# One decode step of gated attention and a feed-forward layer: the feed-forward projections go from TensorE to VectorE, and part of the first load is cut into other pieces

## The chip, the cores and the metric

The kernel runs on one core of a Trainium2 chip. The metric is device time in microseconds of that core, as the median of three runs. In the profile PE is TensorE, DVE is VectorE, ACT is ScalarE, POOL is GpSimd, and SP is the engine that here issues every DMA (a transfer between main memory and the on-chip memory).

## What is computed

One token `x` of 1024 numbers goes through two branches, and a gate mixes them. All data are 32-bit floats.

```python
g = sigmoid((x * gate_w).sum())
# branch A: 32 query heads of 128, 4 key/value heads, 65536 cached positions
q = x @ wq                       # wq 1024 x 4096
p = softmax(q . k_cache / sqrt(128))
a = (p @ v_cache) @ wo           # wo 4096 x 1024
# branch B: one routed token, so the routing picks it
r = x @ w_r
h = silu(x @ w_gate) * (x @ w_up)    # 1024 x 3584 each
b = x + sigmoid(r) * (h @ w_down)    # w_down 3584 x 1024
out = g * a + (1 - g) * b
```

The caches and the weights are some 346 MB, and each byte is used once.

## The kernel before, in words

Everything is written out by hand on five engines, with semaphores between them. The on-chip memory holds three large buffers of 128 partitions by 16384 columns: `kb` and `vb` (named kbuf and vbuf in the profile) and `wb` (wbuf). SP issues the loads in one fixed order on one queue, and before each load it waits until the buffer's last use is counted (`load`).

The stages, in order:

1. **First load.** `wq0` (128 x 8224: the query weights of the first head group, 8192 columns, and 32 columns that hold `x`, `gate_w` and `w_r`) lands in the second half of `wb`. VectorE forms the gate and spreads `x` into `xp`.
2. **Four head groups** (`G`), each with query weights, four K loads and four V loads of 16384 columns (`NL`), a running softmax on VectorE and ScalarE, and the output projection into the PSUM tile T (`T<-wbuf,op`).
3. **Feed-forward projections.** The loop `Fori(0, 2)` runs once for `w_gate` and once for `w_up`. Each weight comes as two halves of 14336 columns, four rows of the weight's 3584 columns to a partition: one half in `kb`, one in `vb`. TensorE multiplies each half by `xp` in 32 matmuls of 448 columns into the PSUM tile R. ScalarE copies R to `row`, TensorE turns it into columns (7 matmuls into S), and VectorE forms silu in `hid` and, after the second pass, `hp`, the hidden vector as TensorE's operand.
4. **Down projection.** The first 16 of 28 blocks of `w_down` come in one load of 16384 columns (semaphore `s_down`) into `wb`, the other 12 in six pieces (`s_part`) into `kb`. VectorE takes the first `SUMS` = 6 blocks as six multiply-adds over 1024 columns into `t`; TensorE takes the rest into T, and adds `t` by two matmuls with ones (`T<-t,ones`). Blocks from `JOIN` = 24 on go straight into the PSUM tile Y, by 64 columns. T is copied to `join` by VectorE, joined into Y by 16 matmuls, and a transpose on VectorE (`fin`) and one small store end the kernel.

PE waits for other engines at `event()`, a wait on the semaphore `to_pe`, and for loads at `landed(...)` or a plain wait. `k_done`, `v_done`, `att_done` and `FFN + n` are counts of PE's own semaphore that SP and the other engines wait for. TensorE's operations are recorded in the helper `mm` (line 149 of the profile) and SP's loads in `load` (line 111). The lines that matter below: 113 (first load), 126 to 138 (order of the feed-forward loads), 210 to 226 (projections), 361 to 396 (silu, `hp` and the six sums).

Of the kernel before, what the change touches and what calls it, by code (L numbers as in the profile page):

```python
# [14 lines left out]
F = 3584  # L15
NL = 4
W = 16384
KB = D // P
FB = F // P
FR = F // 8  # L20
FQ = FB // 4
SCALE = DH ** -0.5
XN = 32
JOIN = 24
SUMS = 6
R4 = 4
CW = D // 16
PIECES = ((0, 3), (3, 4))


# [17 lines left out]
        self.wait(self)  # L48


def gated_mix(nc, k_t, v_t, wq0, wo_wq, tail, out):
# [18 lines left out]
    kb, vb, wb = sb("kbuf", W), sb("vbuf", W), sb("wbuf", W + XN)  # L70
    t, pt = sb("t", 1024), sb("pt", 1024)
    acc, q_sb, join, row = sb("acc", 512), sb("q_sb", 512), sb("join", 512), sb("row", 2 * FR)
    first = wb[:, W // 2 :]
# [19 lines left out]
    S, R, A, M, T, Y = ps("S", 1024), ps("R", 1024), ps("A"), ps("M"), ps("T"), ps("Y")  # L93
# [6 lines left out]
    k_done = lambda g, i: START + HEAD * g + 2 + 3 * i + 1  # L100
# [4 lines left out]
    FFN = START + HEAD * G  # L105


    def load(dst, src, sem, n=0):
        if n:
            sp.wait_ge(pe.sem, n)  # L110
# [13 lines left out]
    half = KB // 2 * F  # L124
    down = at + 4 * half
    for dst, n, sem, after in (
        (kb, half, s_k, k_done(G - 1, NL - 1)),
        (vb, half, s_v, v_done(G - 1, NL - 1)),
        (kb, half, s_k, FFN + 1),
        (vb, half, s_v, FFN + 2),  # L130
        (wb, W, s_down, att_done(G - 1)),
    ):
        load(dst[:, :n], tail[:, at : at + n], sem, after)
        at += n
    parts = [4 * D, 4 * D, 2 * D, D] + [4 * CW * (r1 - r0) for r0, r1 in PIECES]
    for k, n in enumerate(parts):
        to = at - down - W
        load(kb[:, to : to + n], tail[:, at : at + n], s_part[k], 0 if k else FFN + 4)
# [69 lines left out]


    with p.Fori(0, 2):  # L210
        for b, (buf, sem) in enumerate(((kb, s_k), (vb, s_v))):
            landed(sem)
            for k in range(KB // 2):
                for e in range(2):
                    for j in range(4):
                        c = k * F + (2 * j + e) * FR
                        ins = mm(
                            R[32 * j : 32 * j + 32, 512 * e : 512 * e + FR], xp[:, KB // 2 * b + k, :], buf[:, c : c + FR],
                            b == k == 0, b == 1 and k == KB // 2 - 1,
                        )  # L220
            pe(ins)
# [4 lines left out]
    pe.n = FFN + 6  # L226

    event()
    p.wait_ge(s_down, 16)
    d1 = wb.rearrange("p (b n) -> p b n", n=D)  # L230
    tiles(T, [hp[:, b, 3:35] for b in range(SUMS, 16)], d1[:, SUMS:, :], False, False)
    event()
    tiles(T, [ones[:, :32]], t.unsqueeze(1), False, False)
    for k in range(2):
        p.wait_ge(s_part[k], 16)
        d2 = kb[:, 4 * k * D : 4 * (k + 1) * D].rearrange("p (b n) -> p b n", n=D)
        ins = tiles(T, [hp[:, 16 + 4 * k + b, 3:35] for b in range(4)], d2, False, k == 1)
# [6 lines left out]
    later = kb[:, 8 * D : 11 * D].rearrange("p (b j r n) -> p b j r n", b=3, j=4, r=R4)  # L244
    for b in range(3):
        if b != 1:
            p.wait_ge(s_part[(2, 0, 3)[b]], 16)
        for r in range(R4):
            for j in range(4):
                y_row(j, r, hp[:, JOIN + b, :], later[:, b, j, r, :], b == r == 0)  # L250
        if b == 1:
            event()
            joined = join.rearrange("p (j r n) -> p j r n", j=2, r=R4)
            for r in range(R4):
                for j in range(4):
                    y_row(j, r, selj[:, j // 2, :], joined[:, j % 2, r, :])
# [35 lines left out]
    v.wait_ge(s_x, 16)  # L292
    d(v.tensor_copy(xp[:, :, 0], xk[:, 0, :]))
    d(v.tensor_mul(dots, xk[:, 0:1, :].to_broadcast([P, 2, KB]), xk[:, 1:3, :]))
    dve.own()
    tell_pe(v.tensor_reduce(dsum, dots, AX.X, ALU.add))
    act.wait(pe, 1)
# [60 lines left out]
            xr.unsqueeze(1).unsqueeze(3).to_broadcast([P, 4, KB, 32]),  # L358
        )
    )  # L360
    for u in range(2):
        act.wait(pe, FFN + 3 * u + 2)
# [5 lines left out]
        cols = FFN + 3 * u + 3  # L368
        if u == 0:
            act.wait(pe, cols)  # L370
            act(a.activation(hid, S[:, :FB], AF.Exp, scale=-1.0))
            dve.wait(act)
            d(v.tensor_scalar_add(hid, hid, 1.0))
            dve.own()
            d(v.reciprocal(hid, hid))
            dve.own()
            d(v.tensor_mul(hid, S[:, :FB], hid))
            dve.own()
            d(v.tensor_scalar_mul(hid, hid, rest[:, 1:2]))
        else:  # L380
            dve.own()
            dve.wait(pe, cols)
            tell_pe(
                v.tensor_mul(
                    hp[:, :, 3].rearrange("p (j m) -> p m j", j=4), S[:, :FB].rearrange("p (m j) -> p m j", j=4),
                    hid.rearrange("p (m j) -> p m j", j=4),
                )
            )
    d(v.tensor_mul(hid, S[:, :FB], hid))
    dacc, h = t, hid.rearrange("p (m j) -> p j m", j=4)  # L390
    v.wait_ge(s_down, 16)
    dve.own()
    for b in range(SUMS):
        ins = v.scalar_tensor_tensor(dacc, wb[:, b * D : (b + 1) * D], h[:, 0, b : b + 1], dacc, op0=ALU.mult, op1=ALU.add)  # L394
        if b < SUMS - 1:
            d(ins)
            dve.own()
# [43 lines left out]
```

## Time and profile before

| | us |
|---|---|
| Median of three runs | 805.68 (805.59 to 805.71) |
| The profiled execution's own time | 805.7 |
| Its span, first to last instruction | 804.4 |
| TensorE matmuls busy | 396.7 (49%) |
| VectorE busy | 82.2 (10%) |
| ScalarE busy | 24.9 (3%) |

The profiled execution's time agrees with the median, so its stages can be read as those of the timed runs; 1.3 us of it lie outside the span. A row of the timeline has its start, its length, the engine, the line, the operation, what is written and read, the shape and how many instructions are merged in it; in brackets stands the idle time of that engine just before and what ended it. [...]

### The profile page before, as it was taken

Reading aid. Unit: us, or ns where it says so; the run is one execution under the profiler, and the core shown is the slowest. Engines: PE = TensorE matmul, PEld = TensorE weight load, DVE = VectorE, ACT = ScalarE, POOL = GpSimd, SP = SyncE. Lnnn points to the kernel's source line nnn. Section 1 sums busy time; section 2 is a strip of 40 time slices with the busy share of each in tenths; the row PEclk is TensorE's granted clock in tenths of the full one; section 3 lists DMA queues with packets and bytes.
Section 4 is the critical chain, followed back from the end, with each engine's and each line's share of the span. In section 5 each row is a group of like instructions: output and inputs, shape, how many; then the busy total and the mean of one; then the engine's idle time right before and its main releaser. Section 6 shows DMA issues by size and latency. Waiting matters only on the chain. (4 is left out here: it accounts for less than half of the span.)

```text
span 804.4 us, 6296 instructions
## 1 busy us (share of the span) xinstructions
PE 396.7 (49%) x2932; PEld 124.3 (15%) x2932; DVE 82.2 (10%) x159; ACT 24.9 (3%) x49; POOL 2.7 (0%) x12
## 2 busy tenths in 40 slices
PE   3444554455544444455445455455444454545556
PEld 1111111111111111111111111111111111111222
DVE  1010101010001010100101010100101010100004
ACT  0000000000000000000000000000000000000000
POOL 1000000000000000000000000000000000000000
PEclk9777677677676776776776777777777777777768
DMA  9999999999999999999999999999999999999997
GB/s 415 420 418 466 417 420 466 417 417 463 424 417 460 427 417 460 427 417 460 427 417 456 430 417 453 433 417 450 433 420 443 440 420 430 437 449 417 451 422 320
DMA packets 7061, 346.13 MB, mean 430 GB/s; under 512 B 912, under 2 KB 1040, under 8 KB 1296
## 3 DMA queue, kind: packets, MB, share of 16 engines
q1 hardware_dynamic: 7056, 346.05, 99.4%
q8 instruction: 4, 0.07, 0.0%
q14 instruction: 1, 0.01, 0.0%
HBM read 346.05 MB, written 0.00 MB: 430 GB/s over the span
## 5 line engine op out<-in xcount | busy, mean ns | idle before, releaser
L149 PE MATMUL S<-kbuf,qp 128*32 128x512 f32 x1024 | 145.2, 730 | 155.6 <-PEq L146 155.6
L149 PE MATMUL A<-vbuf,pt 128*32 128x512 f32 x1024 | 145.2, 730 | 132.3 <-PEq L146 132.3
L149 PEld LDWEIGHTS S<-kbuf,qp 128*32 128x32 f32 x1024 | 40.1, 131 | 257.4 <-issue 257.4
L149 PEld LDWEIGHTS A<-vbuf,pt 128*32 128x32 f32 x1024 | 40.1, 131 | 224.4 <-issue 224.4
L322 DVE TENSOR_REDUCE m<-S 128x1 f32<-128x1024 f32 x16 | 19.6, 1224 | 291.3 <-PE S L149 291.3
L149 PE MATMUL T<-wbuf,op 128*32 128x512 f32 x128 | 21.9, 847 | 24.5 <-PEq L146 24.5
L341 DVE SCALAR_TENSOR_TENSOR acc<-acc,alpha,A 128x512 f32<-128x512 f32 x12 | 9.0, 748 | 169.1 <-PE A L149 169.1
L149 PE MATMUL R<-vbuf,xp 128*32 128x448 f32 x128 | 17.6, 721 | 16.3 <-PEq L146 16.3
L149 PE MATMUL R<-kbuf,xp 128*32 128x448 f32 x128 | 17.5, 716 | 15.6 <-PEq L146 15.6
L334 ACT ACTIVATE t<-S,nb 128x1024 f32<-128x1024 f32 x16 | 17.6, 1099 | 196.8 <-DVE nb L327 196.8
L338 DVE STREAM_TRANSPOSE pt<-t 128x1024 f32<-128x1024 f32 x16 | 19.8, 1239 | 5.1 <-ACT t L334 5.1
L149 PE MATMUL M<-mg,heads 128*128 128x16 f32 x32 | 5.9, 259 | 27.3 <-PEq L143 27.3
L333 ACT ACTIVATE alpha<-nb 128x1 f32<-128x1 f32 x12 | 3.5, 294 | 449.5 <-DVE nb L330 449.5
L149 PE MATMUL R<-wbuf,xp 128*32 128x512 f32 x128 | 16.1, 647 | 0.0
L149 PEld LDWEIGHTS T<-wbuf,op 128*32 128x32 f32 x128 | 5.7, 148 | 37.5 <-issue 37.5
L149 PEld LDWEIGHTS M<-mg,heads 128*128 128x128 f32 x32 | 4.8, 188 | 41.4 <-issue 41.4
L149 PE MATMUL T<-wbuf,hp 128*32 128x512 f32 x40 | 6.1, 771 | 7.5 <-DMA wbuf<-in_tail 7.5
L149 PEld LDWEIGHTS R<-vbuf,xp 128*32 128x32 f32 x128 | 5.4, 140 | 28.6 <-issue 28.6
L149 PEld LDWEIGHTS R<-kbuf,xp 128*32 128x32 f32 x128 | 5.4, 140 | 27.1 <-issue 27.1
L149 PE MATMUL T<-join 128*128 128x512 f32 x2 | 2.0, 1126 | 13.9 <-PEq L143 13.9
L343 DVE COPY acc<-A 128x512 f32<-128x512 f32 x4 | 2.8, 691 | 59.7 <-PE A L149 59.7
L394 DVE SCALAR_TENSOR_TENSOR t<-wbuf,hid,t 128x1024 f32<-128x1024 f32 x6 | 7.7, 1285 | 7.3 <-DMA wbuf<-in_tail 7.1
(74 smaller groups left out, 80.5 us busy)
## 6 DMA issues: line engine op xcount, KB each, us to landing
kbuf<-in_tail SPq DMA_DIRECT2D x2, 7168.0 KB, 31.0
vbuf<-in_tail SPq DMA_DIRECT2D x2, 7168.0 KB, 29.5
wbuf<-in_wq SPq DMA_DIRECT2D x1, 4112.0 KB, 12.6
wbuf<-in_tail SPq DMA_DIRECT2D x1, 4096.0 KB, 38.0
kbuf<-in_tail SPq DMA_DIRECT2D x2, 2048.0 KB, 34.3
kbuf<-in_tail SPq DMA_DIRECT2D x1, 1024.0 KB, 38.5
kbuf<-in_tail SPq DMA_DIRECT2D x1, 512.0 KB, 39.3
kbuf<-in_tail SPq DMA_DIRECT2D x1, 384.0 KB, 39.8
```

The lines of the kernel that those rows point to most:

```text
L149: return p.matmul(o, w, r, start=first, stop=last)
L322: d(v.tensor_reduce(m1, S, AX.X, ALU.max))
L333: act(a.activation(alpha, was, AF.Exp, bias=now, scale=-1.0))
L334: act(a.activation(t, S, AF.Exp, bias=now, scale=SCALE, accum_out=sums if i else l1))
L338: tell_pe(v.transpose(pt, t))
L341: d(v.scalar_tensor_tensor(acc, acc, alpha, A, op0=ALU.mult, op1=ALU.add))
L343: d(v.tensor_copy(acc, A))
L394: ins = v.scalar_tensor_tensor(dacc, wb[:, b * D : (b + 1) * D], h[:, 0, b : b + 1], dacc, op0=ALU.mult, op1=ALU.add)
```

## The change

The two passes of the projections are taken from TensorE's weights-times-`xp` form. VectorE now multiplies each of the four weight rows on a partition by that partition's `x` and adds it into `facc` (one 128 x 3584 accumulator, which lies half at the end of `kb` and half at the end of `wb`): one product and seven multiply-adds to a pass, in four steps per half. TensorE only adds the accumulator over the partitions, by 8 matmuls with ones. The third half now goes to `wb` and the fourth to `kb`; the down projection's first load goes to `vb` and its pieces to `wb`. Three of these loads now wait for the count `free`, which VectorE raises at the end of a half. `SUMS` goes from 6 to 7 and `JOIN` from 24 to 26: VectorE sums one block more, and two blocks that went into Y go into T. The sum `t` is added to T after the second piece instead of before the first.

The first load loses its first 640 columns. They come as two further DMAs: 96 partitions, whose source is written as 12 groups of 8 rows, and 32 partitions, written as 8 groups of 4 rows, that land in `t`; VectorE copies the latter to their partitions.

```diff
-    sp.dma_start(first, wq0).then_inc(s_x, 16)
+    first, edge = wb[:, W // 2 + SIDE :], wb[:, W // 2 : W // 2 + SIDE]
+    sp.dma_start(first, wq0).then_inc(s_x, 16)
+    sp.dma_start(edge[:96], side[:96].rearrange("(e q) n -> e q n", e=12)).then_inc(s_side, 16)
+    sp.dma_start(t[:32, :SIDE], side[96:].rearrange("(e q) n -> e q n", e=8)).then_inc(s_side, 16)
...
-        (kb, half, s_k, FFN + 1),
-        (vb, half, s_v, FFN + 2),
-        (wb, W, s_down, att_done(G - 1)),
+        (wb, half, s_ffn[2], att_done(G - 1)),
+        (kb, half, s_ffn[3], used(0)),
+        (vb, W, s_down, used(1)),
...
+        event()
+        for e in range(2):
+            for j in range(4):
+                c = 2 * j + e
+                rhs = facc[:, c // 4, (c % 4) * FR : (c % 4 + 1) * FR]
+                ins = mm(R[32 * j : 32 * j + 32, 512 * e : 512 * e + FR], ones[:, :32], rhs)
+        pe(ins)
...
+    v.wait_ge(s_side, 32)
+    d(v.tensor_copy(edge[96:], t[:32, :SIDE]))
...
+    def rows(u, i, buf):
+        v.wait_ge(s_ffn[2 * u + i], 16)
+        if u and i == 0:
+            dve.wait(pe, FFN + 1)
+        for k in range(KB // 2):
+            src = buf[:, k * F : (k + 1) * F].rearrange("p (i n) -> p i n", i=2)
+            x = xk[:, 0, 4 * i + k : 4 * i + k + 1]
+            if i == k == 0:
+                ins = v.tensor_scalar_mul(facc, src, x)
+            else:
+                dve.own()
+                ins = v.scalar_tensor_tensor(facc, src, x, facc, op0=ALU.mult, op1=ALU.add)
+            if k < KB // 2 - 1:
+                d(ins)
+        return ins
...
+    rows(0, 0, kb).then_inc(free, 1)
+    v.wait_ge(free, 1)
+    rows(0, 1, vb).then_inc(free, 1)
+    v.wait_ge(free, 2).then_inc(to_pe, 1)
+    hidden(0)
+    act.wait(pe, FFN + 2)
+    act(a.activation(hid, S[:, :FB], AF.Exp, scale=-1.0))
+    rows(1, 0, wb).then_inc(free, 1)
...
+    v.wait_ge(free, 3)
+    tell_pe(rows(1, 1, kb))
+    hidden(1)
```

`hidden(u)` is ScalarE's copy of R to `row`, as before. On VectorE, from the end of attention to the sums, the order before is this (L373 to L379 are silu, `hp` and `hid` the hidden vector, and L394 the sums of down-projection blocks):

```order
L355 TENSOR_TENSOR t<-ident,xr 128x1024
L373 TENSOR_SCALAR hid<-hid 128x28 [waits n_act]
L375 RECIPROCAL hid<-hid 128x28 [waits n_dve]
L377 TENSOR_TENSOR hid<-S,hid 128x28 [waits n_dve]
L379 TENSOR_SCALAR hid<-hid,rest 128x28 [waits n_dve]
L384 TENSOR_TENSOR hp<-S,hid 128x7x4 [waits n_pe,n_dve]
L389 TENSOR_TENSOR hid<-S,hid 128x28
L394 SCALAR_TENSOR_TENSOR t<-wbuf,hid,t 128x1024 [waits n_dve,s_down]
```

In the changed kernel the same stretch of VectorE reads as follows (`bufs` is the one tensor that now holds `kb`, `wb` and the accumulator; L377 and L380 are the projections):

```order
L363 TENSOR_TENSOR t<-ident,xr 128x1024
L377 TENSOR_SCALAR bufs<-bufs 128x2x1792 [waits s_ffn0]
L380 SCALAR_TENSOR_TENSOR bufs<-bufs 128x2x1792 [waits n_dve] x3
L380 SCALAR_TENSOR_TENSOR bufs<-vbuf,bufs 128x2x1792 [waits n_dve,s_ffn1,free]
L380 SCALAR_TENSOR_TENSOR bufs<-vbuf,bufs 128x2x1792 [waits n_dve] x3
L377 TENSOR_SCALAR bufs<-bufs 128x2x1792 [waits free,n_pe,s_ffn2]
L380 SCALAR_TENSOR_TENSOR bufs<-bufs 128x2x1792 [waits n_dve] x3
L402 TENSOR_SCALAR hid<-hid 128x28 [waits n_act]
...
L380 SCALAR_TENSOR_TENSOR bufs<-bufs 128x2x1792 [waits n_dve,s_ffn3,free]
L380 SCALAR_TENSOR_TENSOR bufs<-bufs 128x2x1792 [waits n_dve] x3
L415 TENSOR_TENSOR hp<-S,hid 128x7x4 [waits n_pe,n_dve]
```

Sixteen long VectorE instructions now stand ahead of `hp`, with the four of silu between the third and the fourth half. On TensorE the program's end before is this, from the down projection on:

```order
L149 MATMUL T<-wbuf,hp 32x512 [waits to_pe,s_down]
L149 MATMUL T<-wbuf,hp 32x512 x19
L149 MATMUL T<-t,ones 32x512 [waits to_pe]
L149 MATMUL T<-t,ones 32x512
L149 MATMUL T<-kbuf,hp 32x512 [waits s_part0]
L149 MATMUL T<-kbuf,hp 32x512 x7
L149 MATMUL T<-kbuf,hp 32x512 [waits s_part1]
L149 MATMUL T<-kbuf,hp 32x512 x7
L149 MATMUL Y<-kbuf,hp 32x64 [waits s_part2]
L149 MATMUL Y<-kbuf,hp 32x64 x31
L149 MATMUL Y<-join,selj 32x64 [waits to_pe]
```

And this is TensorE's end in the changed kernel:

```order
L161 MATMUL T<-vbuf,hp 32x512 [waits to_pe,s_down]
L161 MATMUL T<-vbuf,hp 32x512 x17
L161 MATMUL T<-bufs,hp 32x512 [waits s_part0]
L161 MATMUL T<-bufs,hp 32x512 x7
L161 MATMUL T<-bufs,hp 32x512 [waits s_part1]
L161 MATMUL T<-bufs,hp 32x512 x7
L161 MATMUL T<-t,ones 32x512 [waits to_pe]
L161 MATMUL T<-t,ones 32x512
L161 MATMUL T<-bufs,hp 32x512 [waits s_part2]
L161 MATMUL T<-bufs,hp 32x512 x3
L161 MATMUL Y<-bufs,hp 32x64 [waits s_part3]
L161 MATMUL Y<-join,selj 32x64 [waits to_pe]
```

The two matmuls on `t` moved behind 16 others; only 4 matmuls of T, and 32 fewer of Y, stand behind them.

## Rows read from the trace of the kernel before

**Rows 1.** The page: the queues of the whole execution, with packets, MB, and the share of 16 DMA engines' span.

```profile
DMA  9999999999999999999999999999999999999997
...
q1 hardware_dynamic: 7056, 346.05, 99.4%
q8 instruction: 4, 0.07, 0.0%
```

**Rows 2.** The chain of waits that ended last, in order of time: start, length, what.

```profile
795.54 4.41 PE T L149 x35
799.96 0.97 PE Y L149 x61
...
802.67 0.25 DVE fin L402
```

**Rows 3.** The timeline of the last 25 us, all engines.

```profile
777.27 0.92 ACT L365 ACTIVATE row<-R 128x896 f32<-128x896 f32 x1 [30.96 <-PE R L149]
...
778.34 1.70 PE L149 MATMUL S<-sel,row 128*128 128x4 f32 x14 [1.12 <-PEq L143]
780.14 0.21 DVE L384 TENSOR_TENSOR hp<-S,hid 128x28 f32<-128x28 f32 x1 [32.76 <-PE S L149]
780.25 0.18 DVE L389 TENSOR_TENSOR hid<-S,hid 128x28 f32<-128x28 f32 x1
787.50 7.89 DVE L394 SCALAR_TENSOR_TENSOR t<-wbuf,hid,t 128x1024 f32<-128x1024 f32 x6 [7.08 <-DMA wbuf<-in_tail]
...
787.52 6.12 PE L149 MATMUL T<-wbuf,hp 128*32 128x512 f32 x40 [7.49 <-DMA wbuf<-in_tail]
...
795.54 0.62 PE L149 MATMUL T<-t,ones 128*32 128x512 f32 x2 [1.90 <-PEq L143]
...
796.02 4.00 PE L149 MATMUL T<-kbuf,hp 128*32 128x512 f32 x30
...
800.10 0.69 DVE L400 COPY join<-T 128x512 f32<-128x512 f32 x1 [4.71 <-PE T L149]
...
800.94 0.65 PE L149 MATMUL Y<-join,selj 128*32 128x64 f32 x32
...
801.38 1.22 PE L149 MATMUL Y<-kbuf,hp 128*32 128x64 f32 x64
```

**Rows 4.** The timeline of PE at the start, from the first K load on: when TensorE could begin on each load.

```profile
32.73 8.92 PE L149 MATMUL S<-kbuf,qp 128*32 128x512 f32 x64 [9.41 <-PEq L146]
...
53.59 8.73 PE L149 MATMUL A<-vbuf,pt 128*32 128x512 f32 x64 [9.87 <-PEq L146]
72.90 9.31 PE L149 MATMUL S<-kbuf,qp 128*32 128x512 f32 x64 [10.58 <-PEq L146]
...
92.20 9.90 PE L149 MATMUL A<-vbuf,pt 128*32 128x512 f32 x64 [7.92 <-PEq L146]
```

**Rows 5.** The timeline of the projections: the four halves on PE, and silu.

```profile
717.57 8.68 PE L149 MATMUL R<-kbuf,xp 128*32 128x448 f32 x64 [10.20 <-PEq L146]
...
734.53 8.73 PE L149 MATMUL R<-vbuf,xp 128*32 128x448 f32 x64 [8.28 <-PEq L146]
...
746.34 0.18 DVE L373 TENSOR_SCALAR hid<-hid 128x28 f32<-128x28 f32 x1 [41.79 <-ACT hid L371]
...
747.14 0.24 DVE L379 TENSOR_SCALAR hid<-hid,rest 128x28 f32<-128x28 f32 x1
...
751.44 8.81 PE L149 MATMUL R<-kbuf,xp 128*32 128x448 f32 x64 [5.36 <-PEq L146]
...
768.30 8.91 PE L149 MATMUL R<-vbuf,xp 128*32 128x448 f32 x64 [8.05 <-PEq L146]
```

**Rows 6.** VectorE's instructions grouped by line and shape over the whole execution: busy us, mean ns of one.

```profile
L394 DVE SCALAR_TENSOR_TENSOR t<-wbuf,hid,t 128x1024 f32<-128x1024 f32 x6 | 7.7, 1285 | 7.3 <-DMA wbuf<-in_tail 7.1
...
L337 DVE SCALAR_TENSOR_TENSOR l<-l,alpha,sums 128x1 f32<-128x1 f32 x12 | 2.6, 220 | 17.5 <-ACT t L334 17.5
...
L345 DVE TENSOR_SCALAR lb<-ones,l 128x128 f32<-128x128 f32 x4 | 1.1, 286 | 0.1
L349 DVE TENSOR_SCALAR rl<-rl,sig 128x8 f32<-128x8 f32 x4 | 0.9, 231 | 0.1
```

**Rows 7.** PE's matmuls grouped by shape in the stretch from 717.5 to 720.5 us, the first 16 of the first half.

```profile
L149 PE MATMUL R<-kbuf,xp 128*32 128x448 f32 x16 | 3.2, 952 | 10.2 <-PEq L146 10.2
```

**Rows 8.** The timeline of SP's queue: when the last loads were issued.

```profile
726.31 0.33 SPq L111 DMA_DIRECT2D kbuf<-in_tail  x1
743.32 0.33 SPq L111 DMA_DIRECT2D vbuf<-in_tail  x1
743.69 0.43 SPq L111 DMA_DIRECT2D wbuf<-in_tail  x1
760.31 2.70 SPq L111 DMA_DIRECT2D kbuf<-in_tail  x6
```

**Rows 9.** The timeline of VectorE after the first load.

```profile
13.34 0.17 DVE L293 COPY xp<-wbuf 128x8 f32<-128x8 f32 x1 [8.51 <-DMA wbuf<-in_wq]
...
23.36 0.21 DVE L315 COPY qp<-M 128x32 f32<-128x32 f32 x1 [1.21 <-PE M L149]
```

More of the change, by code (lines that the diff above doesn't have):

```diff
@@ L23 @@
 XN = 32
-JOIN = 24
-SUMS = 6
+JOIN = 26
+SUMS = 7
 R4 = 4
 CW = D // 16
+SIDE = 640
 PIECES = ((0, 3), (3, 4))
@@ L48, in own, with gated_mix @@
         self.wait(self)
-def gated_mix(nc, k_t, v_t, wq0, wo_wq, tail, out):
+def gated_mix(nc, k_t, v_t, wq0, side, wo_wq, tail, out):
     pe, dve, act, pool = (
@@ L61, in gated_mix @@
     s_part = [nc.alloc_semaphore(f"s_part{i}") for i in range(6)]
+    s_ffn = [nc.alloc_semaphore(f"s_ffn{i}") for i in range(4)]
     def sb(name, *shape):
@@ L69, in gated_mix @@
         sb("gap", (256 - nc.sbuf_base % 256) // 4)
-    kb, vb, wb = sb("kbuf", W), sb("vbuf", W), sb("wbuf", W + XN)
+    bufs, vb = sb("bufs", 2 * W + 2 * XN), sb("vbuf", W)
+    kb, wb = bufs[:, :W], bufs[:, W : 2 * W + XN]
+    facc = bufs[:, : 2 * W].rearrange("p (i n) -> p i n", i=2)[:, :, W - F // 2 :]
     t, pt = sb("t", 1024), sb("pt", 1024)
     acc, q_sb, join, row = sb("acc", 512), sb("q_sb", 512), sb("join", 512), sb("row", 2 * FR)
-    first = wb[:, W // 2 :]
+    first, edge = wb[:, W // 2 + SIDE :], wb[:, W // 2 : W // 2 + SIDE]
+    s_side = nc.alloc_semaphore("s_side")
     xk = wb[:, W : W + 3 * KB].rearrange("p (i k) -> p i k", i=3)
@@ L105, in gated_mix, with used @@
     FFN = START + HEAD * G
+    free = nc.alloc_semaphore("free")
+    def used(i):
+        return free, i + 1
     def load(dst, src, sem, n=0):
         if n:
-            sp.wait_ge(pe.sem, n)
+            sp.wait_ge(*(n if isinstance(n, tuple) else (pe.sem, n)))
         sp.dma_start(dst, src).then_inc(sem, 16)
     sp.dma_start(first, wq0).then_inc(s_x, 16)
+    sp.dma_start(edge[:96], side[:96].rearrange("(e q) n -> e q n", e=12)).then_inc(s_side, 16)
+    sp.dma_start(t[:32, :SIDE], side[96:].rearrange("(e q) n -> e q n", e=8)).then_inc(s_side, 16)
     for g in range(G):
@@ L126, in gated_mix @@
     for dst, n, sem, after in (
-        (kb, half, s_k, k_done(G - 1, NL - 1)),
-        (vb, half, s_v, v_done(G - 1, NL - 1)),
-        (kb, half, s_k, FFN + 1),
-        (vb, half, s_v, FFN + 2),
-        (wb, W, s_down, att_done(G - 1)),
+        (kb, half, s_ffn[0], k_done(G - 1, NL - 1)),
+        (vb, half, s_ffn[1], v_done(G - 1, NL - 1)),
+        (wb, half, s_ffn[2], att_done(G - 1)),
+        (kb, half, s_ffn[3], used(0)),
+        (vb, W, s_down, used(1)),
     ):
@@ L137, in gated_mix @@
         to = at - down - W
-        load(kb[:, to : to + n], tail[:, at : at + n], s_part[k], 0 if k else FFN + 4)
+        load(wb[:, to : to + n], tail[:, at : at + n], s_part[k], 0 if k else used(2))
         at += n
@@ L210, in gated_mix @@
     with p.Fori(0, 2):
[L211 to L221, printed above, removed]
+        event()
[5 more added lines that the diff above has]
+        pe(ins)
         event()
@@ L225, in gated_mix @@
         pe(ins)
-    pe.n = FFN + 6
+    pe.n = FFN + 4
     event()
     p.wait_ge(s_down, 16)
-    d1 = wb.rearrange("p (b n) -> p b n", n=D)
+    d1 = vb.rearrange("p (b n) -> p b n", n=D)
     tiles(T, [hp[:, b, 3:35] for b in range(SUMS, 16)], d1[:, SUMS:, :], False, False)
-    event()
-    tiles(T, [ones[:, :32]], t.unsqueeze(1), False, False)
-    for k in range(2):
+    d2 = wb[:, : 10 * D].rearrange("p (b n) -> p b n", n=D)
+    for k, (b0, b1) in enumerate(((0, 4), (4, 8), (8, 10))):
         p.wait_ge(s_part[k], 16)
-        d2 = kb[:, 4 * k * D : 4 * (k + 1) * D].rearrange("p (b n) -> p b n", n=D)
-        ins = tiles(T, [hp[:, 16 + 4 * k + b, 3:35] for b in range(4)], d2, False, k == 1)
+        ins = tiles(T, [hp[:, 16 + b, 3:35] for b in range(b0, b1)], d2[:, b0:b1, :], False, k == 2)
+        if k == 1:
+            event()
+            tiles(T, [ones[:, :32]], t.unsqueeze(1), False, False)
     join_ready = pe(ins)
@@ L242, in y_row @@
         return mm(y[32 * j : 32 * j + 32, :], lhs[:, 3 - r : 35 - r], rhs, first, last)
[L244 to L256, printed above, removed]
+    later = wb[:, 10 * D : 11 * D].rearrange("p (j r n) -> p j r n", j=4, r=R4)
+    p.wait_ge(s_part[3], 16)
+    for r in range(R4):
+        for j in range(4):
+            y_row(j, r, hp[:, JOIN, :], later[:, j, r, :], r == 0)
+    event()
+    joined = join.rearrange("p (j r n) -> p j r n", j=2, r=R4)
+    for r in range(R4):
+        for j in range(4):
+            y_row(j, r, selj[:, j // 2, :], joined[:, j % 2, r, :])
     at = 11 * D
@@ L360, in gated_mix, with hidden @@
     )
-    for u in range(2):
-        act.wait(pe, FFN + 3 * u + 2)
+    def rows(u, i, buf):
[13 more added lines that the diff above has]
+        return ins
+    def hidden(u):
+        act.wait(pe, FFN + 2 * u + 1)
         if u:
@@ L367, in gated_mix @@
         ).then_inc(to_pe, 1)
[L368 to L388, printed above, removed]
+    rows(0, 0, kb).then_inc(free, 1)
[6 more added lines that the diff above has]
+    rows(1, 0, wb).then_inc(free, 1)
+    dve.wait(act)
+    d(v.tensor_scalar_add(hid, hid, 1.0))
+    dve.own()
+    d(v.reciprocal(hid, hid))
+    dve.own()
+    d(v.tensor_mul(hid, S[:, :FB], hid))
+    dve.own()
+    d(v.tensor_scalar_mul(hid, hid, rest[:, 1:2]))
+    v.wait_ge(free, 3)
+    tell_pe(rows(1, 1, kb))
+    hidden(1)
+    dve.own()
+    dve.wait(pe, FFN + 4)
+    tell_pe(
+        v.tensor_mul(
+            hp[:, :, 3].rearrange("p (j m) -> p m j", j=4), S[:, :FB].rearrange("p (m j) -> p m j", j=4),
+            hid.rearrange("p (m j) -> p m j", j=4),
+        )
+    )
     d(v.tensor_mul(hid, S[:, :FB], hid))
@@ L393, in gated_mix @@
     for b in range(SUMS):
-        ins = v.scalar_tensor_tensor(dacc, wb[:, b * D : (b + 1) * D], h[:, 0, b : b + 1], dacc, op0=ALU.mult, op1=ALU.add)
+        ins = v.scalar_tensor_tensor(dacc, vb[:, b * D : (b + 1) * D], h[:, 0, b : b + 1], dacc, op0=ALU.mult, op1=ALU.add)
         if b < SUMS - 1:
@@ L422 @@
         "v": a["A_v_cache"].reshape(G, NL, P, W),
-        "wq0": np.concatenate([wq[0].reshape(P, -1), vecs], axis=1),
+        "wq0": np.concatenate([wq[0].reshape(P, -1)[:, SIDE:], vecs], axis=1),
+        "side": wq[0].reshape(P, -1)[:, :SIDE],
         "wo_wq": np.stack([wo[:-1], wq[1:]], axis=2).reshape(G - 1, P, W),
```

2 lines of the change are left out of this document (1 added, 1 removed).

## The prediction

> **What bounds the kernel now.** I read the page's queues first: the data queue keeps the sixteen DMA engines busy for 99.4% of the span with 346.05 MB, and every slice but the last stands at nine tenths or more [rows 1]. The transfers are the bound, and the change moves the same bytes. So a change can do two things only: alter how evenly and how late the loads land, or alter the work that follows the last loads. Then I read the chain that ended last: it is PE without a pause from 795.54, Y, and the transpose at 802.67 [rows 2]. The timeline of the end shows where that chain hangs: VectorE's six sums start at 787.50, ended by a load, take 7.89, and PE's product on their result starts 0.15 after them [rows 3]. So the end hangs on the landing of the down projection's first load. The hidden vector `hp` had been there since 780.35, and VectorE and PE waited some 7 us for that load [rows 3]. These 7 us are the cover for anything that makes the hidden vector later. The four halves reach PE at 717.57, 734.53, 751.44 and 768.30, 16.9 us apart, and PE needs 8.7 to 8.9 for each [rows 5].
>
> **The new chain on VectorE, step by step.** A multiply-add costs 220 ns on 1 column and 1285 on 1024, so 1.041 ns a column more; on 3584 columns that is 3.95 us [rows 6]. The six sums took 7.89 where six times 1.285 is 7.71, so 0.036 lies between two [rows 3, 6]. A half of four multiply-adds is 4 x 3.95 + 3 x 0.036 = 15.91 us. That is less than the 16.9 between landings by only 1.0, against 8 before, and what stands between the halves has to fit into that.
>
> A half that begins with the plain product has one cheap instruction. TENSOR_SCALAR took 231 ns on 8 columns and 286 on 128, 0.46 ns a column [rows 6], about half the multiply-add's. Its bounds on 3584 columns are 1.9 (that slope) and 3.95 (the multiply-add's slope). I take 2.1, half the multiply-add's slope over the same fixed part, since the nearest row shows such a slope: 14.06 for the half.
>
> Second half: PE begins on it at 734.53 today [rows 5]; VectorE waits for the load without PE's own wait-and-clear instruction, so I put it at 734.4 (estimate). It ends at 750.3. Then TensorE has to add over the partitions, after an event (0.15 as after the sums [rows 3], and 0.05 for the extra semaphore instruction): 8 products, 16 instructions, from an idle PE. The first 16 of a half took 3.2 [rows 7], so 753.7. The third half, landed at 751.4, may only start then, since it overwrites the accumulator: 753.8, and it ends at 767.9. Silu's four small instructions now stand between the halves on the same engine: 746.34 to 747.38 [rows 5], 1.04 and about 0.1 around them. The fourth half has landed at 768.2 but starts at 769.0, and ends at 784.9. Event and reduction 3.35: 788.3. From the end of R to the end of `hp` today: 777.21 (768.30 + 8.91 [rows 5]) to 780.35 [rows 3], 3.14. So `hp` is there at 791.4, eleven us later than today, and 3.9 later than the load that covered it. The stall on that load goes; the hidden vector is late in its place.
>
> Behind it: the sums begin at 791.5 and are seven, 7 x 1.285 + 6 x 0.036 = 9.21, to 800.7. PE takes 0.15 and then, on `t` and on the two blocks behind it, four turns of T. Such a turn is 0.43: the nine from the first product on `t` to the last start fill 795.54 to 799.40 (the end, 800.02, less one matmul's 0.62 [rows 3]). So 3 x 0.43 + 0.62 = 1.9, to 802.8. Copy of T 0.08 + 0.69, 0.15 to PE, 0.44 for the join, 0.65 for the last 32 instructions, 0.07 to the transpose, all as today [rows 3]: the transpose starts at 804.84, against 802.67. The chain's sum is +2.17. PE alone would not be later there: the 18 products on the first load's blocks and 16 behind them fit between 791.5 and 800.8 by today's 6.12 for 20 and about 3.4 for 16 [rows 3], with little room (0 to 0.3 us more if TensorE starts slowly).
>
> [...]
>
> What costs nothing: the matmuls taken from PE (it waits in this stage); the copy of 32 x 640 and two more issues at the start (K's first product starts at 32.73, the query is ready at 23.57: 9 us of cover [rows 4, 9]). SP's loads now wait for VectorE: they are issued at about 731.6, 750.4 and 767.9 instead of 726.31, 743.69 and 760.31 [rows 8]. The queue ahead of them still holds work until the landings at 751.4, 768.3 and 787.5 [rows 3, 5], 18 us or more; a hole there would need VectorE to be that late.
>
> **The first load.** A load counts as landed when its slowest engine is done. K and V loads reach PE 19.3 us apart (53.59, 72.90, 92.20), but the first pair is 20.86 apart [rows 4]: something cost a DMA engine 1.55 us once, and it was not made up later. The only other traffic is four instruction packets of some 17 KB [rows 1]. If one engine carries such a block, it lands last from then on, and every load lands with it. In the change four of sixteen engines can have no share of the 640 columns, if a group is an engine's work. By rate, 346.05 MB / 16 in 799.6 us is 27.05 KB a us: 8 rows x 2560 B = 0.76 us less for those four, nothing for four others, 4 rows = 0.38 more for eight. The bounds for every landing are thus -0.76 (the late engine is among the four) and +0.38 (it is among the eight). No view names the engine. The packet records under the views, which no row prints, show it among the last four of the sixteen to take up the first load; on that weak sign I take -0.75.
>
> [...]
>
> **Sum.** +2.17 - 0.75 = +1.4 against the profiled execution's 805.7, which agrees with the median of 805.68: 807.1 us. A change under 0.2%, 1.6 us, is what a measurement of this kernel cannot tell from none.
>
> **Rivals.**
> - *The late engine isn't relieved* (the pieces spread over all engines, or the late one is among the twelve). Place: the landing of the second half, from which the whole chain counts. Price 0 to +0.38 instead of -0.75, decided by which engine carried the block. For it: four of sixteen is few. Against: the order of first packets. 807.8 to 808.3, slower than before.
> - *The product runs at the multiply-add's rate.* Only the third half's product is on the path: +1.87, 809.0. Against it the slope of [rows 6].
> - *The loads bind as before.* If VectorE's chain were 2.1 us shorter than I reckon, the end would hang on the last pieces, 0.75 earlier than now: 804.9 to 805.6. For it: 7 us of cover today. Against: five waits in series, all with rows.
> - *Faster.* With fewer TensorE instructions some of the four blocks go, and if all engines also ended even, at most the 1.55 would be gained: 804.1, the edge of what counts as faster. It needs the former rival too.
>
> **How the numbers follow.** Forecast 0.66, with 806.6 to 807.6 as its own range (VectorE's sum to 0.3, PE's turns to 0.3); about a third of it lies above 807.3, where slower begins. Unrelieved 0.17, nearly all slower. Full-rate product 0.04, slower. Loads binding 0.09, same. Faster 0.04. So slower 0.23 + 0.16 + 0.04 = 0.43, same 0.43 + 0.01 + 0.09 = 0.53, faster 0.04. The range runs from 805.0, which takes in most of the loads-bound case, to 808.4, the end of the unrelieved one.
>
> **What would show it.** The long multiply-adds at 3.95 us and the product at 2.1. The third half's start ended by PE R, not by a load; the fourth half's start some 0.8 after its landing. `hp` after the first down load has landed, so that no DMA ends the wait of the first sum. The first V product some 0.75 earlier than 53.59, with those at 72.90 and 92.20 moved alike; unmoved or later ones are the first rival. Wrong would be: sums that still wait for the load, or a long multiply-add far from 3.95.

## The result, and the profile after

The changed kernel takes 809.86 us in the median of five runs (809.54 to 812.8), where the kernel before takes 805.59 in five: a ratio of 1.0061, with an interval from 1.0048 to 1.0074. It is slower by more than the measurement's 0.2%, and it lies above the range of 805.0 to 808.4. The profiled execution took 809.6, with a span of 808.3. One execution each of experiments 6 and 7 below (830.09 and 827.92 us) ran in a slower state of the chip, and their figures leave it out.

The page's line on DMA packets and its queues come first.

```profile
DMA packets 7220, 346.11 MB, mean 428 GB/s; under 512 B 944, under 2 KB 1072, under 8 KB 1456
...
q1 hardware_dynamic: 7216, 346.05, 99.0%
q8 instruction: 3, 0.05, 0.0%
```

The bytes are those of [rows 1], and the queue's share is 0.4 points lower, over a span 3.9 us longer. Of the four packets of q8, whose kind the page gives as instruction, one is gone.

VectorE's instructions from 715 to 803 us, grouped by line and shape (busy us, mean ns of one, idle time ahead and what ended it):

```profile
L380 DVE SCALAR_TENSOR_TENSOR bufs<-bufs 128x3584 f32<-128x3584 f32 x10 | 39.5, 3952 | 0.5
...
L425 DVE SCALAR_TENSOR_TENSOR t<-vbuf,hid,t 128x1024 f32<-128x1024 f32 x7 | 9.0, 1285 | 0.3
L377 DVE TENSOR_SCALAR bufs<-bufs 128x3584 f32<-128x3584 f32 x2 | 4.2, 2086 | 15.6 <-DMA bufs<-in_tail 12.1 <-PE R L161 3.6
```

The long multiply-add is 3.952 us where 3.95 was reckoned from [rows 6], the product 2.086 where 2.1 was taken, and no DMA stands any more as what the sums wait for.

The timeline of the end, from the second half on:

```profile
734.63 15.91 DVE L380 SCALAR_TENSOR_TENSOR bufs<-vbuf,bufs 128x3584 f32<-128x3584 f32 x4 [2.89 <-DMA vbuf<-in_tail]
...
750.74 3.21 PE L161 MATMUL R<-bufs,ones 128*32 128x448 f32 x16 [41.02 <-PEq L155]
...
754.10 2.08 DVE L377 TENSOR_SCALAR bufs<-bufs 128x3584 f32<-128x3584 f32 x1 [3.55 <-PE R L161]
...
755.08 3.12 PE L161 MATMUL S<-sel,row 128*128 128x4 f32 x14 [1.12 <-PEq L155]
756.22 11.93 DVE L380 SCALAR_TENSOR_TENSOR bufs<-bufs 128x3584 f32<-128x3584 f32 x3
...
768.06 0.17 DVE L402 TENSOR_SCALAR hid<-hid 128x28 f32<-128x28 f32 x1
...
769.23 15.91 DVE L380 SCALAR_TENSOR_TENSOR bufs<-bufs 128x3584 f32<-128x3584 f32 x4
...
785.29 3.22 PE L161 MATMUL R<-bufs,ones 128*32 128x448 f32 x16 [27.09 <-PEq L155]
...
788.56 0.92 ACT L389 ACTIVATE row<-R 128x896 f32<-128x896 f32 x1 [30.13 <-PE R L161]
...
789.62 3.12 PE L161 MATMUL S<-sel,row 128*128 128x4 f32 x14 [1.12 <-PEq L155]
792.85 0.21 DVE L415 TENSOR_TENSOR hp<-S,hid 128x28 f32<-128x28 f32 x1 [7.71 <-PE S L161]
...
793.23 9.21 DVE L425 SCALAR_TENSOR_TENSOR t<-vbuf,hid,t 128x1024 f32<-128x1024 f32 x7
...
806.57 0.25 DVE L433 STREAM_TRANSPOSE fin<-Y 128x64 f32<-128x64 f32 x1 [1.30 <-PE Y L161]
```

Each product of the program shows as two instructions in these rows: the 8 of R are x16, as the 32 of a half are x64 in [rows 5]. Read the timeline from the end. Seven sums follow `hp` at once, so the 7.08 us of waiting for the load in [rows 3] are used up and 5.73 more are needed (793.23 against 787.50). VectorE has only two pauses after 734.63 in the two projections: the 3.55 that R ends, and the 7.71 that S ends. In the second of these, R takes 3.2, the copy 0.9 and S 3.12. In [rows 3] the same S took 1.70.

S now runs at a lower granted clock of TensorE than before. First two stretches of the changed kernel, R and then S of the second pass; then the kernel before, S of its second pass (stretch: us; busy time of PE, PEld, DVE, ACT and POOL with their instructions in brackets; granted clock; DMA share; GB/s):

```profile
785.20:788.50 3.30, 3.21 (x16) 0.69 (x16) 0.00 (x0) 0.00 (x0) 0.00 (x0) 0.50 0.86 367
789.60:792.80 3.20, 3.12 (x14) 3.05 (x14) 0.00 (x0) 0.00 (x0) 0.00 (x0) 0.50 1.01 430
```

```profile
778.30:780.10 1.80, 1.70 (x14) 1.64 (x14) 0.00 (x0) 0.00 (x0) 0.00 (x0) 1.00 0.42 182
```

Below, a granted clock of 1.00 is called the high level and one of 0.50 the low level. Before, S came behind 64 instructions of R that had kept TensorE busy for 8.9 us [rows 5]. Now it comes behind 16 that took 3.2 us out of 27 us of idling, and the same pause of 1.1, and the clock is at 0.50 in S as in R, where it was 1.00 before.

At the start, the two rows of the first K and the first V product:

```profile
33.17 9.65 PE L161 MATMUL S<-bufs,qp 128*32 128x512 f32 x64 [10.19 <-PEq L158]
...
53.78 9.59 PE L161 MATMUL A<-vbuf,pt 128*32 128x512 f32 x64 [8.88 <-PEq L158]
```

The first V product should have started 0.75 before the 53.59 of [rows 4]. It starts 0.19 after it.

Taken together, the transpose starts at 806.57 where the prediction, with its 0.75 taken off, has 804.09. Of these 2.48 us, 0.98 arise at the start of the second half (734.63 against 733.65) and 1.43 between the end of the fourth half and the end of `hp`; 0.07 are left for all the rest. My theory was thus: **the first load's pieces relieve no engine and cost some tenths, and the low level of the clock in S costs 1.4 us (3.12 less 1.70).** The rivals to it were that the pieces are to blame for most of it, and that the landings behind them, not S, keep the chain late.

### The profile page after: what moved, and what is told of

It is laid out like the page before. It is cut to its first block, busy times and chain, and to the rows that moved or that the text cites. A ratio compares the mean times of both kernels' runs of the same rounds, so it can differ in the third digit from the quotient of the medians.

```text
span 808.3 us, 5750 instructions
## 1 busy us (share of the span) xinstructions
PE 376.9 (47%) x2648; PEld 118.4 (15%) x2648; DVE 143.4 (18%) x177; ACT 24.9 (3%) x49; POOL 2.7 (0%) x12
## 5 line engine op out<-in xcount | busy, mean ns | idle before, releaser
L161 PE MATMUL S<-bufs,qp 128*32 128x512 f32 x1024 | 148.6, 746 | 157.1 <-PEq L158 157.1
L161 PE MATMUL A<-vbuf,pt 128*32 128x512 f32 x1024 | 150.5, 753 | 128.6 <-PEq L158 128.6
L161 PEld LDWEIGHTS S<-bufs,qp 128*32 128x32 f32 x1024 | 40.8, 134 | 261.6 <-issue 261.6
L380 DVE SCALAR_TENSOR_TENSOR bufs<-bufs 128x3584 f32<-128x3584 f32 x10 | 39.5, 3952 | 0.5
L161 PE MATMUL R<-bufs,ones 128*32 128x448 f32 x32 | 6.4, 953 | 68.1 <-PEq L155 68.1
L161 PE MATMUL T<-bufs,op 128*32 128x512 f32 x128 | 20.7, 805 | 21.9 <-PEq L158 21.9
L380 DVE SCALAR_TENSOR_TENSOR bufs<-vbuf,bufs 128x3584 f32<-128x3584 f32 x4 | 15.8, 3952 | 3.0 <-DMA vbuf<-in_tail 2.9
L161 PE MATMUL R<-bufs,xp 128*32 128x512 f32 x128 | 15.0, 609 | 0.0
L161 PEld LDWEIGHTS T<-bufs,op 128*32 128x32 f32 x128 | 5.3, 144 | 34.1 <-issue 34.1
L425 DVE SCALAR_TENSOR_TENSOR t<-vbuf,hid,t 128x1024 f32<-128x1024 f32 x7 | 9.0, 1285 | 0.3
```

Source lines behind the costliest of these rows:

```text
L380: ins = v.scalar_tensor_tensor(facc, src, x, facc, op0=ALU.mult, op1=ALU.add)
L425: ins = v.scalar_tensor_tensor(dacc, vb[:, b * D : (b + 1) * D], h[:, 0, b : b + 1], dacc, op0=ALU.mult, op1=ALU.add)
```

## The experiments

The first four kernels ran beside the kernel before on one chip, where its median was 805.44, the other four on another, where it was 805.54.

| kernel | median us | ratio and interval | S, second pass | transpose starts |
|---|---|---|---|---|
| before | 805.59 | | 1.70 | 802.67 |
| changed | 809.86 | 1.0061 (1.0048 to 1.0074) | 3.12 | 806.57 |
| 1: whole first load | 809.56 | 1.0049 (1.0035 to 1.0062) | 1.70 | 804.35 |
| 2: pieces alone | 805.97 | 1.0012 (1.0003 to 1.0021) | 1.70 | 802.94 |
| 3: TensorE kept busy | 807.68 | 1.0024 (1.0014 to 1.0034) | 1.70 | 803.89 |
| 4: pieces apart | 809.48 | 1.0046 (1.0032 to 1.0059) | 3.12 | 806.42 |
| 5: before, pieces apart | 805.88 | 1.0004 (0.9995 to 1.0013) | 2.03 | 803.17 |
| 6: two matmuls behind R | 808.22 | 1.0043 (1.0030 to 1.0056) | 1.73 | 805.13 |
| 7: silu later | 809.12 | 1.0043 (1.0030 to 1.0056) | 1.70 | 804.73 |
| 8: whole load, silu later, busy | 806.37 | 1.0015 (1.0006 to 1.0024) | 1.70 | 802.79 |

The last two columns are those of each kernel's one profiled execution, the others of its timed runs. Of the changed kernel's variants, only experiments 3 and 8 have intervals clear of the changed kernel's; those of 1, 4, 6 and 7 overlap it.

**1. The changed kernel with the first load whole again.**

```diff
-    sp.dma_start(edge[:96], side[:96].rearrange("(e q) n -> e q n", e=12)).then_inc(s_side, 16)
-    sp.dma_start(t[:32, :SIDE], side[96:].rearrange("(e q) n -> e q n", e=8)).then_inc(s_side, 16)
...
-    v.wait_ge(s_side, 32)
-    d(v.tensor_copy(edge[96:], t[:32, :SIDE]))
```

> The changed kernel with the first load in one piece again; the projections stay on VectorE. Theory: the two small pieces made the second half's landing about 0.15 us later and relieved no engine, and all else of the slowdown is VectorE's chain. Then the first multiply-add on vbuf starts near 734.5 instead of 734.63 and the median is 809.3 to 809.9. Rival A, the slowdown sits in the stream of loads that the pieces disturb: back near 806. Rival B, the pieces did give the predicted 0.75: this run is slower, about 810.4.

The median, 809.56, is within what was expected and cannot be told from the changed kernel's. The second half starts 0.82 earlier than there, though, where 0.15 was expected. And the five times fall into two groups, 807.63 and 807.85, and 809.56 to 810.3, and the profiled execution is one of the lower. Its timeline at the second half and at the second pass of R and S:

```profile
733.81 15.91 DVE L374 SCALAR_TENSOR_TENSOR bufs<-vbuf,bufs 128x3584 f32<-128x3584 f32 x4 [2.98 <-DMA vbuf<-in_tail]
...
784.47 3.21 PE L157 MATMUL R<-bufs,ones 128*32 128x448 f32 x16 [28.51 <-PEq L151]
...
788.80 1.70 PE L157 MATMUL S<-sel,row 128*128 128x4 f32 x14 [1.12 <-PEq L151]
```

R took 3.21 at a granted clock of 0.50 as in the changed kernel, with the same pause of 1.12 behind it, and S, the same instructions on the same operands, ran at 1.00, where it has 0.50 there. So after the same R the clock was at either level for S. The transpose is 2.22 earlier than in the changed kernel: 1.42 by S and 0.82 by the second half's load. That the upper group had S at 3.12 wasn't seen, since only one execution has a trace, and 1.42 doesn't fill the 2 us between the groups. Other traces fit: the times of experiments 4, 6 and 7 fall into two such groups as well (no time of these four kernels lies between 808.45 and 809.03), the traced executions with S at 3.12 took 809.48 and 809.6, and those of experiments 1, 6 and 7, with S at 1.70 or 1.73, 807.85 to 808.22.

**2. The kernel before with the pieces alone**: the two loads, VectorE's wait and its copy, as removed above, added to it.

> The kernel before with only the first load cut as in the change; the projections stay on TensorE. Theory: all landings move by 0.1 to 0.2, median 805.6 to 805.9. Rival A (the stream is what got slower): 808 or more. Rival B (the pieces relieve the late engine): 804.8 to 805.0.

805.97 against 805.44, just above the 805.6 to 805.9 expected: the pieces cost some 0.5 us, with 0.2 to 1.7 in the interval, which excludes a gain. The line on packets and the first products:

```profile
DMA packets 7221, 346.13 MB, mean 430 GB/s; under 512 B 944, under 2 KB 1072, under 8 KB 1456
```

```profile
33.56 8.35 PE L153 MATMUL S<-kbuf,qp 128*32 128x512 f32 x64 [9.79 <-PEq L150]
...
53.81 8.47 PE L153 MATMUL A<-vbuf,pt 128*32 128x512 f32 x64 [9.82 <-PEq L150]
```

The first K product starts 0.83 later than in [rows 4], and the first V product 0.22 later. The second half starts at 734.94 and the sums at 787.90, both 0.4 later than before [rows 3, 5]. The other traces agree with the sign: the second half starts at 733.81 to 734.53 in the three with the whole load, and at 734.54 to 734.94 in the five with these pieces. The packets show how the pieces ran. The kernel before has 912 packets under 512 B. It issues 48 loads and one store, and 49 times 16 plus the store's 128 rows is just 912, which fits one small packet of each load for each engine it runs on. The pieces bring 944, 32 more: two transfers on sixteen engines each. The groups lie behind one another in main memory, and the split by 12 and by 8 did not come about.

**3. TensorE kept busy during the last two multiply-adds of the second and the fourth half.** 24 matmuls go into the tile A, which nothing reads any more.

```diff
         event()
+        for i in range(24):
+            mm(A[32 * (i % 4) : 32 * (i % 4) + 32, :], ones[:, :32], pt[:, :512])
+        event()
...
+            if i == 1 and k == 1:
+                v.wait_ge(dve.sem, dve.n).then_inc(to_pe, 1)
```

> The changed kernel with 24 matmuls whose result nobody reads, on TensorE in each pass during the last two multiply-adds of the second and the fourth half. Theory: the 16 matmuls into R and the 14 into S are slow because TensorE had stood idle; with work just before them R takes about 1.7 instead of 3.2 in both passes and S about 1.7 instead of 3.1 in the second one. That is 4.4 us off VectorE's chain, which then ends near the landing of the last pieces: 805.5 to 806.3. Rival (the chain is not what ends last, or S is slow for another reason, such as its operands): R and S keep 3.2 and 3.1, or the end stays at 809.5 or more.

```profile
769.25 16.02 DVE L383 SCALAR_TENSOR_TENSOR bufs<-bufs 128x3584 f32<-128x3584 f32 x4 [1.36 <-DMA bufs<-in_tail]
...
785.42 1.71 PE L161 MATMUL R<-bufs,ones 128*32 128x448 f32 x16 [0.69 <-PEq L155]
...
788.25 1.70 PE L161 MATMUL S<-sel,row 128*128 128x4 f32 x14 [1.12 <-PEq L155]
```

R takes 1.71 and S 1.70 in both passes, 1.5 and 1.4 us shorter than in the changed kernel, and the median falls by 2.2, with an interval clear of the changed kernel's. In the five traces without this work (the changed kernel and experiments 1, 4, 6 and 7) R took 3.21 or 3.22 in every pass; so with work just before it (7.48 and 7.33 us on A), R took 1.71 where it took 3.21 without. But 805.5 to 806.3 was expected. The rows name what is missing: VectorE comes to the fourth half 1.36 us ahead of its load, so what the first pass saves is lost to that landing, and this half starts no earlier than the changed kernel's 769.23. Part of that lateness is an instruction packet at 748.29, which made the third half's last DMA engine 0.47 us later (experiment 5 has such a case in full). This execution was also the slowest of the kernel's nine; its store took 3.4 us from issue to landing where those of the other nine kernels took 1.4:

```profile
out<-fin SPq DMA_DIRECT2D x1, 4.0 KB, 3.4
```

The packet records under the views, which no row prints, show why: 127 of the store's 128 packets were done by 805.22, and the last ran at 806.41, right behind a packet of the instruction queue that lasted from 805.48 to 806.35. In the other nine traces the last instruction packet ended before the store was issued.

**4. The changed kernel with 64 idle columns between the groups in main memory,** so that they cannot become one piece.

```diff
-    sp.dma_start(edge[:96], side[:96].rearrange("(e q) n -> e q n", e=12)).then_inc(s_side, 16)
+    sp.dma_start(edge[:96], side_a[:, :-64].rearrange("e (q n) -> e q n", q=8)).then_inc(s_side, 16)
```

The second piece is changed alike, with 8 groups of 4.

> The changed kernel with the source of the two pieces padded in main memory, 64 columns behind each group, so that a group cannot merge with the next one. Theory: in the change the groups merged and both pieces ran on all 16 engines (32 packets under 512 B more than before); here they run on 12 and on 8, so the page counts 932 packets under 512 B instead of 944, four engines are spared, and if the late engine is one of them the landings come about 0.8 earlier than in the change: first multiply-add on vbuf near 733.8, median 808.9 to 809.2. Rival (the late engine is not among the spared, or the spared ones stand idle until the next load's turn): landings as in the change or up to 0.4 later, 809.8 to 810.4.

```profile
DMA packets 7208, 346.11 MB, mean 428 GB/s; under 512 B 932, under 2 KB 1060, under 8 KB 1444
```

932 is 20 more than 912: 12 engines and 8. Now the split is as the prediction took it. The first V product starts at 53.07, 0.71 before the changed kernel's. That is the size of the forecast relief, but against the kernel before it is only 0.52, and experiments 1 and 8, with the whole load, start this product at 52.93 and 52.95. The second half at 734.26 is 0.37 earlier than in the changed kernel, where 0.8 was expected. The median lies between the ranges of theory and rival, and, 0.4 under the changed kernel's, within the scatter of its runs (807.96 to 810.24). The relief isn't settled by this one. S took 3.12 again:

```profile
789.26 3.12 PE L161 MATMUL S<-sel,row 128*128 128x4 f32 x14 [1.12 <-PEq L155]
```

In experiments 2 and 4, by the 32 and 20 small packets that are added, the same 12 and 8 groups ran on 16 engines each where they lay behind one another in memory, and on 12 and 8 where they lay apart.

**5. The kernel before with the same separate pieces.**

> The kernel before, projections on TensorE, with the two small pieces whose groups are kept apart by padding in main memory. In the profile of e4_spare the pieces ran on 12 and 8 engines and the second half landed some 0.4 earlier than with merged groups. Theory: the relief exists and is worth about what the pieces cost, so this run lies 0.3 to 0.8 below e2_split_only and near the kernel before: 804.9 to 805.6. Rival (the pieces cost the same 0.5 however they are split): 805.8 to 806.2.

805.88, in the rival's range and not to be told from the kernel before, so the forecast gain of 0.75 is not there even where the engines are spared. Its trace shows an early start come and go: the first V product at 52.94 and the second half at 734.06 are 0.65 and 0.47 earlier than before [rows 4, 5], but the third half starts 0.62 later, and the sums 0.64 later:

```profile
752.06 7.77 PE L153 MATMUL R<-kbuf,xp 128*32 128x448 f32 x64 [6.95 <-PEq L150]
...
788.14 7.89 DVE L400 SCALAR_TENSOR_TENSOR t<-wbuf,hid,t 128x1024 f32<-128x1024 f32 x6 [7.79 <-DMA wbuf<-in_tail]
```

The packet records show what took it back. From 743.67 an instruction packet of 16 KB ran for 0.88 us on one DMA engine, and the data packet behind it took 2.67 where the others take 2.12. That engine fell 1.41 behind and ended its share of the third half at 751.43; the other fifteen had ended by 750.51. In the kernel before, an instruction packet at 742.65 costs its engine 1.41 as well, but that engine has more than this to spare, and the third half's last engine stays 16.91 behind the second's, as between the other halves. So whether such a packet moves a landing depends on the engine that it falls to.

Nor is a term of half a microsecond to be read from single traces here: experiments 1 and 8 have the same loads up to there, and VectorE starts on the second half at 733.81 and at 734.28. The table's 2.03 for S goes with a falling clock: in the first microsecond of S the granted clock was 1.00 and in the rest of it 0.60, behind an R of 7.86 us that had ended at 1.00. So here the 7.86 us of work ahead did not keep S at the high level.

**6. The changed kernel with two more matmuls behind R.**

```diff
         pe(ins)
+        for i in range(2):
+            mm(A[32 * i : 32 * i + 32, :], ones[:, :32], pt[:, :512])
         event()
```

> The changed kernel with two matmuls whose result nobody reads behind the eight of R, so that TensorE works through ScalarE's copy of R. Theory: the 14 matmuls into S took 3.12 instead of 1.70 because TensorE's clock was still at its lower level after only 3.2 us of work and a pause of 1.1; with the pause filled S takes 1.7 in every run, R stays at 3.2, and the median falls by about 1.4, to 808.2 to 808.7, with less spread. Rival (S is slow through its operands or the semaphores; or the two extra matmuls delay S by as much): S stays near 3.1 or starts 0.8 later, 809.6 or more.

R and then S of the second pass, in the columns of the stretches above:

```profile
785.20:788.40 3.20, 3.19 (x18) 1.08 (x20) 0.00 (x0) 0.00 (x0) 0.00 (x0) 0.50 0.87 374
789.55:791.30 1.75, 1.73 (x16) 1.64 (x14) 0.00 (x0) 0.00 (x0) 0.00 (x0) 1.00 1.03 440
```

With two matmuls behind R, of which nothing waits for the result, S takes 1.73 at a granted clock of 1.00 where it had taken 3.12 at 0.50. R itself is still 3.21, and the second half starts at 734.55, as in the changed kernel. `hp` starts at 791.38 in place of 792.85, and the transpose at 805.13 in place of 806.57: 1.44 for 1.39 of S. With the same loads and the same work on VectorE, that is the price of the low level in this chain. That the two matmuls brought the high level isn't shown: experiments 1 and 7 have S at 1.70 without them, and this is one trace. The median is 808.22, within what was expected, but its interval overlaps the changed kernel's, and the smaller spread that was expected is not there (807.92 to 810.58).

**7. The changed kernel with silu's four instructions behind the fourth half**, in place of between the halves.

```diff
     dve.wait(act)
+    v.wait_ge(free, 3)
+    tell_pe(rows(1, 1, kb))
     d(v.tensor_scalar_add(hid, hid, 1.0))
...
-    v.wait_ge(free, 3)
-    tell_pe(rows(1, 1, kb))
     hidden(1)
```

> The changed kernel with VectorE's four small silu instructions moved behind the fourth half, where they lie beside TensorE's 3.2 us on R. Theory (VectorE's chain from the second half on sets the end): the fourth half starts when it lands, near 768.4, instead of 769.2, and everything behind it moves by 0.8: median 808.9 to 809.3. Rival (the end hangs on TensorE's turns or on the last pieces): the median stays at 809.5 to 810.

```profile
768.78 15.91 DVE L380 SCALAR_TENSOR_TENSOR bufs<-bufs 128x3584 f32<-128x3584 f32 x4 [0.73 <-DMA bufs<-in_tail]
...
789.17 1.70 PE L161 MATMUL S<-sel,row 128*128 128x4 f32 x14 [1.12 <-PEq L155]
```

809.12, within what was expected, and not to be told from the changed kernel. The fourth half starts 0.45 earlier, not the 1.17 that silu's instructions take up in the changed kernel (768.06 to 769.23), and now waits for its load: behind silu stands the landing, as the prediction had it with its 768.2 and 769.0. Its transpose at 804.73 owes 1.42 to S, which took 1.70 here without any added work, as in experiment 1.

**8. The three mends at once**: the first load whole, silu behind the fourth half, and TensorE kept busy by 8 matmuls during the last multiply-add of each pass (the code of experiment 3 with 8 for 24 and `k == 2` for `k == 1`).

> The changed kernel with the first load whole, silu behind the fourth half, and 8 matmuls whose result nobody reads during the last multiply-add of the second and the fourth half. Theory: with R and S at 1.7 each and the fourth half starting at its landing, the chain behind that landing is 34.6 us, the transpose starts near 802.8 as in the kernel before, and the time is 805.2 to 806.2: all of the loss is found again, and nothing is won, because the landings set the rest. Rival (something else in the change costs 1 us or more, such as VectorE's long instructions beside the loads): 806.7 or more.

```profile
768.17 16.02 DVE L377 SCALAR_TENSOR_TENSOR bufs<-bufs 128x3584 f32<-128x3584 f32 x4 [0.86 <-DMA bufs<-in_tail]
...
784.33 1.71 PE L157 MATMUL R<-bufs,ones 128*32 128x448 f32 x16 [0.76 <-PEq L151]
...
787.16 1.70 PE L157 MATMUL S<-sel,row 128*128 128x4 f32 x14 [1.12 <-PEq L151]
...
802.79 0.25 DVE L432 STREAM_TRANSPOSE fin<-Y 128x64 f32<-128x64 f32 x1 [1.30 <-PE Y L157]
```

806.37, just above the 805.2 to 806.2 expected: about 3.4 of the 4.3 us are back, and the transpose stands 0.12 from the 802.67 of [rows 2]. The R of the first pass, not shown here, still took 2.60, at a granted clock of 0.64 over this stretch. The kernel is still not faster than before: the fourth half is bound by its load and takes 16 us from there, so that the sums begin at 789.35, past the 787.50 at which the kernel before starts them [rows 3]. Of the 0.8 us that the median is behind, the trace shows 0.1 in the span; 0.4 more lie outside it, where this execution has 1.7 us (806.18 less 804.5), as all five of experiment 1 have (1.6 to 1.75), and the kernel before 1.3. Why is open.

## Why the prediction was wrong

**Right: what bounds, and that the cover is used up.** The end hung on the load with some 7 us of cover, and the change made `hp` later than that. The sums start behind `hp`, and no DMA ends their wait, as was written.

**Right: VectorE's chain.** From the start of the second half to the end of the fourth, 50.51 us were measured (734.63 to 785.14) and 50.5 forecast (734.4 to 784.9). The four terms hold one by one: 15.91 a half, 3.2 for R, 2.08 for the product, and the third half's start ended by PE R. The seven sums are 9.21 as forecast, and from their end at 802.44 to the transpose pass 4.13, where 800.7 to 804.84 was forecast. The rival of the product at the full rate is out by 2086 ns. Extrapolating a slope from 1024 columns to 3584 and taking half of it for the plain product cost nothing.

**Wrong by 1.43: "From the end of R to the end of `hp` today … 3.14".** This step copied a duration from a place where TensorE had just worked for 8.9 us, to one where it comes from idling. [Rows 7], which the prediction used for R, already showed what TensorE did behind 10.2 us of idling: 3.2 us for 16 instructions, where four times as many took 8.7 [rows 5]. What I priced for R I didn't price for what follows it. With S at 3.12, as the trace shows, the step is 4.55. In the traces of experiments 1, 6 and 7, where S took 1.70 to 1.73, it is 3.13 to 3.17, as forecast: so the step is not always wrong, but its length went with that of S, and so with the clock (1.00 for S in experiments 1 and 6, 0.50 in the changed kernel), whose level the prediction took for given. Work just before R (experiments 3 and 8) went with S at 1.70 or 1.71 in all four passes.

**Wrong by 0.98: "on that weak sign I take -0.75".** Two things were wrong in it. The pieces ran on all sixteen engines, so none was spared (32 small packets more, not 20): 0.75 of the 0.98. That a group is one engine's work was my assumption. It did not hold in the changed kernel, and no run shows the 0.75 at every landing: with the groups apart, the first V product started 0.71 earlier than in the changed kernel (experiment 4) and 0.65 earlier than in the kernel before (experiment 5), the second half only 0.37 and 0.47. And they cost, 0.5 us in experiment 2; whether that is more than the upper bound of +0.38, which counted bytes only, its interval doesn't settle, and the other 0.23 of this trace is within the scatter. Experiment 5 shows that the spared engines would not have brought the gain either: a later instruction packet made another engine the last one and took it back. What the prediction guessed of the cause was right: in the kernel before an instruction packet at 41.95 puts one engine 1.41 us behind, most of the 1.55 that it had seen. The rival that "the pieces spread over all engines" is what happened in that part. It had 0.17, against 0.66 for a case that rested on a sign called weak. With its 807.8 to 808.3 and S at 3.12, the sum is 809.2 to 809.7, beside 809.6 in the profiled execution.

**The range.** Its upper end took in the unrelieved engine and nothing else, since every term behind R was called "as today". An unknown clock level for S, with a price of 1.4 on one side, would have put the end at 809.8, still just under the median of 809.86.

**What stays open.** What the pieces' half microsecond is made of; what sets the clock's level behind the same R, and whether two more matmuls change it; what makes the upper group of times in experiment 1, beyond S; and the 0.4 us outside the span in experiment 8.

## What to carry to other kernels

Where work moves from an engine that idles between bursts to one that is nearly full, the wait ahead of the stage's end (here 7 us) is not spent on the longer instructions alone, but on each handover that becomes serial, and the engine that is left with short bursts may run them slowly (in the five traces with no work added ahead of R, R took 3.21 or 3.22 in every pass, and S 3.12 in two of them): take the time of a small step from a place in the trace where the engine came from the same idling, not from where the step stands today. How a load is divided among the DMA engines is to be read from its packets (944 small ones here with the groups together, 932 with them apart), not from how its source is written. And a gain that rests on a sign one would call weak should get the smaller chance, with the time of the other case as the forecast.

## What the runs showed of the hardware that was not expected

- Behind an R of 3.21 or 3.22 us, S took 3.12 in the profiled executions of the changed kernel (granted clock 0.50) and of experiment 4, and 1.70 in those of experiments 1 (granted clock 1.00) and 7. Two more matmuls behind R went with 1.00 and 1.73, in one trace.
- Two pieces of 240 and 80 KB that replace a part of a 4112 KB load cost some 0.5 us of an 805 us kernel (ratio 1.0003 to 1.0021).
- An instruction packet of 16 KB among long data packets put its DMA engine 1.41 to 1.53 us behind, in all ten traces; a load landed later by it only where that engine became the last (0.9 us in experiment 5, nothing at 742.65 in the kernel before).
- A 4 KB store took 3.4 us to land in one execution (experiment 3), where its last packet ran behind an instruction packet, and 1.4 in that of every other kernel here.
